# The early TensorE order written out by hand, first values by a one-hot matmul, and w_in loaded by columns

## The chip, the cores and the metric

The kernel runs on one core of a Trainium2 chip. The metric is the device time of one execution in microseconds (us); smaller is better. The four runs of the kernel before took 231.32, 231.59, 231.93 and 228.98 us, with a median of 231.45 us.

## What is computed

Attention over a sliding window with a few sink tokens, followed by a feed-forward layer. Four sequences (batches) of 768 tokens, eight heads of 64 columns. Each query sees the 128 keys up to its own position and the first four keys of its sequence. The result, 3072 tokens by 512 columns, goes through a gated layer with 2048 hidden columns. Cut to what matters:

```
scores = (q @ k.T) / sqrt(64)
keep   = (key < 4) | ((0 <= query - key) & (query - key < 128))
a      = softmax(where(keep, scores, -1e9))
x      = concat_heads(a @ v)                  # 3072 x 512
h      = x @ w_in                             # 3072 x 2048
g      = h * sigmoid(beta * h)
out    = g @ w_out                            # 3072 x 512
```

All inputs and the output are float32 in HBM; the kernel casts to bfloat16 for its matmuls.

## The kernel before

**Units.** The work is cut into eight half batches of 384 tokens (`hb`), and each into four head pairs. A pair of one half batch is a unit `u`, 32 of them, `u = 4 * hb + pair`. For a unit the kernel does these steps, each a group of instructions on TensorE with its followers on other engines:

- `T(u)` (L594): six transposes of q and k, 128 by 128, into one PSUM bank, and one copy of 768 columns to `qkT`, by ScalarE (ACT) or VectorE (DVE).
- `SC(n)` (L657): a burst of score matmuls. Each tile covers two PSUM banks; an exponential of 1024 columns on ACT writes `E`, and masks zero what may not be seen: for blocks with sink columns a product with `maskS` on DVE or GpSimd (POOL), for diagonal and previous blocks an `affine_select` of 512 columns on POOL (L703). One burst of each half batch also holds the scores of the sink keys for all four units (`SS`, L710), with an exponential into `ES`.
- `AV(u)` (L736): probabilities times values, 65 columns a matmul (64 values and a one that gives the denominator). Queries that lie beyond the first blocks take the sinks by one matmul of `ES` with `vS` (L746). A reciprocal and a product on DVE normalise (L761, L763).
- `OT(u)` (L769): three transposes of the result and a copy to `xT`.
- `HQ(T_, m)` (L793): for one token half `T_` and one of 16 chunks of 128 hidden columns, four matmuls of 384 columns, a tanh on ACT (L806) and a gate product on DVE (L808). Below, H0, H1 and so on are these in order.
- `OQ(T_, t, j)` (L815): four matmuls of 512 columns, a quarter of one output tile; after the fourth quarter a copy and a store. Below, O.

In the rest of the text T4, S5, A4, R4 are `T(4)`, `SC(5)`, `AV(4)` and `OT(4)`.

**First values.** `vS` holds the values of the four sink tokens, placed so that each head only meets its own rows. `load_first` (L552) fetches them from HBM in four loads of 8 KB for all batches, into a buffer zeroed by POOL (L468); `first_values` (L557) multiplies by the 0/1 array `own` on DVE, once for each batch.

**Loads.** All come from the SyncE (SP) queue, in program order. q and k of half batch 0 come in four loads of two heads each, those of half batches 1 and 2 in one load each of 768 KB; v in three loads of 256 KB with rows of 256 bytes. Weights come in 16 loads of 512 KB: `load_w(j)` (L512) for j < 8 takes half the depth of w_in and 512 of its columns (rows of 2 KB), for j >= 8 two row blocks of w_out. `cast_w(j)` casts on ACT, DVE or POOL, whichever the planner finds free first. An H therefore waits for two loads. The list is in L844: half batch 0, half batch 1, all weights, then the rest. The sink values' loads are put in after half batch 0.

**Order.** The program adds its operations to a graph; half batch 0 in an order written out (L979 to L1002), the rest by a loop (L1009 on) that picks the next group by expected readiness. `Graph.arrange` (L124) then plans every engine's queue from written-in durations: TensorE's next group is the earliest ready of the first `SKIP` = 3 in the list. While half batch 0 waits, filler matmuls of `ones` (L1003) go in. PSUM has eight banks; `take` gives the run of banks that is free first. The queues are fixed when the kernel is built, and TensorE works strictly in its order.

## Time and profile before

| | us |
|---|---|
| median of four runs | 231.45 |
| the profiled execution | 231.32 |
| its span, first to last instruction | 229.4 |
| TensorE (PE) busy | 215.4 (94%) |
| ACT busy | 142.8 (62%) |
| DVE busy | 139.2 (61%) |
| POOL busy | 65.3 (28%) |
| SP queue's transfers, share of the 16 DMA engines' span | 73.2% |
| H matmuls, 512 of 384 columns, busy | 95.1 |
| O matmuls, 360 records of 512 columns, busy | 90.3 |
| fillers, 54, busy (1.1 to 19 us) | 9.8 |

Times in the profile are counted from the start of the span. Matmuls overlap in their pipeline, so the mean duration of one (326 ns for H's) is longer than the distance from one start to the next. The chain that ended last lies on TensorE for 83% of the span, on transfers of k for 6%, on ACT for 4%. A line of a timeline gives the start, the length, the engine, the code line, the operation, the output and input with shapes, the count, and in brackets how long the engine sat idle before it and who ended that. The slices are fortieths of the span, 5.7 us each; a digit is a busy share in tenths.

### The profile page before, as it was taken

What the parts mean: (1) busy time and instruction counts of PE and PEld (TensorE: products, weight loads), DVE (VectorE), ACT (ScalarE), POOL (GpSimd) and SP (SyncE); (2) the same over time, 40 slices, a digit from 0 to 9 for tenths busy, and PEclk for the clock granted to TensorE, in tenths of its full rate; (3) what the DMA queues carried; (4) which work ended last, traced back from release to release, by engine and by line L of the source; (5) the groups of instructions that cost most, each with busy time, mean ns of one, the idle gap of its engine ahead of it and who ended that gap; (6) DMA issues with size and microseconds to landing.
All of it is one profiled execution on the core that took longest, in us unless ns stands there. A gap on an engine that the chain in (4) does not pass through costs nothing.

```text
span 229.4 us, 4562 instructions
## 1 busy us (share of the span) xinstructions
PE 215.4 (94%) x1771; PEld 125.3 (55%) x1795; DVE 139.2 (61%) x293; ACT 142.8 (62%) x226; POOL 65.3 (28%) x118
## 2 busy tenths in 40 slices
PE   7974989999899999999999999999999999999993
PEld 5662666554546456555655555656555565555541
DVE  2794559997686356567966563776765554533310
ACT  2844897775881487827667479672767864744421
POOL 5463493003262044407200046360120750000000
PEclk9997699999999999999999999999999999999999
DMA  6969699999985996987746995999669523011112
GB/s 168 244 197 334 175 357 367 334 300 236 197 199 113 246 237 96 201 197 148 153 87 160 223 212 96 225 189 163 135 117 209 182 80 83 0 46 49 47 48 90
DMA packets 95158, 39.79 MB, mean 174 GB/s; under 512 B 81809, under 2 KB 87969, under 8 KB 95137
## 3 DMA queue, kind: packets, MB, share of 16 engines
q1 hardware_dynamic: 95136, 39.51, 73.2%
q8 instruction: 14, 0.23, 0.4%
q14 instruction: 8, 0.06, 0.1%
HBM read 27.30 MB, written 6.29 MB: 146 GB/s over the span
## 4 chain that ended last, share of the span: by engine, by line
PE 83%; DMA 6%; ACT 4%; DVE 2%; issue 1%; SPq 1%; POOL 1%
PE P L801 36%; PE P L821 35%; DMA k_stage<-in_k_dram 6%; PE P L757 4%; PE P L678 4%; ACT E L690 2%; PE P L602 2%; PE P L746 1%; ACT qkT L444 1%; SPq L554 1%; DVE w_in L449 1%; POOL E L703 1%; DVE g L808 1%; PE P L783 1%; DVE k L449 1%
## 5 line engine op out<-in xcount | busy, mean ns | idle before, releaser
L806 ACT ACTIVATE t<-P,hbeta 128x384 f32<-128x384 f32 x128 | 72.9, 585 | 39.3 <-PE P L801 31.2
L808 DVE SCALAR_TENSOR_TENSOR g<-t,P 128x384 bf16<-128x384 f32 x128 | 68.7, 549 | 46.5 <-ACT t L806 43.4
L801 PE MATMUL P<-xT,w_in 128*128 128x384 bf16 x512 | 95.1, 326 | 0.7 <-ACT E L690 0.5
L821 PE MATMUL P<-w_out,g 128*128 128x512 bf16 x360 | 90.3, 379 | 1.7 <-issue 0.6
L703 POOL TENSOR_SCALAR_AFFINE_SELECT E<-E 128x512 bf16<-128x512 bf16 x72 | 48.8, 705 | 78.5 <-ACT E L690 78.4
L801 PEld LDWEIGHTS P<-xT,w_in 128*128 128x128 bf16 x512 | 48.2, 98 | 37.4 <-DVE w_in L449 0.9
L821 PEld LDWEIGHTS P<-w_out,g 128*128 128x128 bf16 x384 | 36.5, 98 | 36.4 <-DVE w_out L449 0.3
L690 ACT ACTIVATE E<-P 128x1024 bf16<-128x1024 f32 x44 | 43.0, 1031 | 10.2 <-PE P L678 9.9
L444 ACT ACTIVATE osb<-P 128x512 f32<-128x512 f32 x19 | 11.4, 599 | 20.1 <-PE P L821 19.6
L763 DVE TENSOR_TENSOR onorm<-P,rden 128x384 bf16<-128x384 f32 x32 | 17.8, 556 | 1.0
L757 PE MATMUL P<-vaug,E 128*128 128x65 bf16 x352 | 17.1, 193 | 0.2 <-POOL E L703 0.2
L757 PEld LDWEIGHTS P<-vaug,E 128*128 128x128 bf16 x352 | 15.6, 97 | 2.4 <-POOL E L703 0.3
L678 PE MATMUL P<-qkT 64*128 64x128 bf16 (+1 forms) x288 | 14.9, 237 | 0.6 <-ACT E L690 0.3
L678 PEld LDWEIGHTS P<-qkT 64*128 64x128 bf16 x288 | 9.8, 97 | 8.3 <-issue 2.6
L746 PE MATMUL P<-vS,ES 128*128 128x130 bf16 x64 | 12.8, 220 | 1.5 <-DVE vS L560 1.1
L449 DVE CAST k<-k_stage 128x512 bf16<-128x512 f32 (+1 forms) x19 | 9.6, 511 | 6.7 <-DMA k_stage<-in_k_dram 6.7
L761 DVE RECIPROCAL rden<-P 128x6 f32<-128x6 f32 x32 | 6.0, 188 | 10.9 <-PE P L757 10.8
L446 POOL TENSOR_SCALAR_AFFINE_SELECT q<-q_stage 128x512 bf16<-128x512 f32 x6 | 4.8, 814 | 26.1 <-DMA q_stage<-in_q_dram 26.1
L449 DVE CAST vaug<-v_stage 128x512 bf16<-128x512 f32 x21 | 9.9, 474 | 3.2 <-DMA v_stage<-in_v_dram 3.2
L1003 PE MATMUL P<-ones 128*128 128x256 bf16 x54 | 9.8, 331 | 1.1 <-POOL ones L455 1.1
L444 ACT ACTIVATE qkT<-P 128x768 bf16<-128x768 bf16 x9 | 7.0, 811 | 6.1 <-PE P L602 6.1
L698 DVE TENSOR_TENSOR E<-E,maskS 128x512 bf16<-128x512 bf16 x16 | 9.1, 580 | 2.3 <-ACT E L690 2.1
(50 smaller groups left out, 93.3 us busy)
## 6 DMA issues: line engine op xcount, KB each, us to landing
v_stage<-in_v_dram SPq DMA_DIRECT2D x24, 256.0 KB, 4.4
out_dram<-osb SPq DMA_DIRECT2D x24, 256.0 KB, 2.4
q_stage<-in_q_dram SPq DMA_DIRECT2D x15, 256.0 KB, 4.9
k_stage<-in_k_dram SPq DMA_DIRECT2D x15, 256.0 KB, 4.9
wst<-in_moe_w_in_dram SPq DMA_DIRECT2D x5, 512.0 KB, 9.3
wst<-in_moe_w_out_dram SPq DMA_DIRECT2D x4, 512.0 KB, 4.5
g<-in_moe_w_out_dram SPq DMA_DIRECT2D x4, 512.0 KB, 5.2
q_stage<-in_q_dram SPq DMA_DIRECT2D x2, 768.0 KB, 6.6
```

What stands on the lines that cost most here:

```text
L444: return lambda e: e.activation(dst, src, AF.Copy, bias=0.0, scale=scale)
L449: return lambda e: e.tensor_copy(dst, src)
L678: add("pe", lambda e, dst=dst, kt=kt, kc=kc, rows=rows, q0=q0, nq=nq, u=u: e.matmul(dst, kt[rows, kc:kc + 128], qkT[rows, u % NT, 0, q0:q0 ...
L690: add("act", lambda e, src=src, dst_=dst_: e.activation(dst_, src, AF.Exp, bias=0.0, scale=SCALE), act_ns(1024), w=[("E", z)] + [("m", z, ...
L703: add("gp", lambda e, dd=dd, sg=sg: e.affine_select(dd, dd, [[0, 4], [sg, 128]], ALU.is_ge, 0.0, base=min(sg, 0), channel_multiplier=-sg), ...
L746: add("pe", lambda e, m=m, c0=c0: e.matmul(A[:, c0:c0 + 2 * (D + 1)], ES[u // 4 % 2][:, m * 128:(m + 1) * 128], vS[b % 2][:, 2 * hp:2 * hp ...
L757: e.matmul(A[:, c0:c0 + D + 1], E[t_ % NE][:, i, hh, :], vaug[vz][:, kb % NK, 2 * hp + hh, :], start=a, stop=o, skip_group_check=True), 31,
L763: add("dve", lambda e: e.tensor_tensor(onorm[on][:, :, :, :].rearrange("p m h d -> p (m h) d"), av[:, :, 0:D], rden[on][:, :].unsqueeze(2) ...
L801: add("pe", lambda e, c=c: e.matmul(hp, w_in16[:, c, m * 128:(m + 1) * 128], xT[:, c, t0:t0 + HALF], start=(c == 0), stop=(c == 3)), mm_ns ...
L806: add("act", lambda e: e.activation(tt[ti][:, :], hp, AF.Tanh, bias=0.0, scale=hbeta[:, m:m + 1]), act_ns(HALF) + 93, r=["hbeta"], w=[("t" ...
L808: add("dve", lambda e: e.scalar_tensor_tensor(gt[T_ % NG][:, m, :], tt[ti][:, :], 1.0, hp, ALU.add, ALU.mult), dve_ns(HALF), r=[("t", ti)] ...
L821: add("pe", lambda e, m=m: e.matmul(P[:, bk, :], gt[T_ % NG][:, m, t * 128:(t + 1) * 128], w_out16[:, m, :], start=(m == 0), stop=(m == NM ...
```

## The change

Six things change.

1. **The early order.** For half batch 0 the list is T0 T1 S0 T2 S1 T3 S4 S2, the first values, S3, then A0 A1 R0 A2 R1 A3 R2 R3. After it stands a new written list of H, T and S for the next stage. For the first 60 us of the plan `arrange` may choose among ten groups, not three. In the resulting TensorE order H0 to H7 directly follow R3, then T4 to T7, then H8, S5, H9, and so on; the last part of the order, from the last attention unit on, is as before. PSUM banks of this stage are dealt out from written lists (`ring`, `two`).
2. **First values of batch 0** by one matmul with the 0/1 matrix `sel` from the values that are already in the vaug buffer; the product with `own` then reads PSUM. For batches 1 to 3 one load of 32 KB each, later in the queue.
3. **w_in loads** take the full depth and 256 columns (rows of 1 KB), so that an H waits for one load. w0, w1, w2 go ahead of half batch 1's q, w3 between its q and k, w4 and w5 between k and v; the `chain` argument keeps the order. beta's load moves behind w1. The first three casts have a fixed engine.
4. **T for the first two half batches** uses two banks and two copies of 384 columns.
5. **Diagonal and previous masks** of units 0 to 7 may also run on DVE, as a product with `maskT`.
6. **Output tiles of token half 0** go quarter by quarter over three tiles, and q and k heads 4 to 7 of half batch 0 come in one load each.

The diff, cut to its core:

```
     SKIP = 3
+    WIDE, EARLY = 10, 60000
...
-            for i, grp in enumerate(todo_pe[:self.SKIP]):
+            for i, grp in enumerate(todo_pe[:self.SKIP if self.free["pe"] > self.EARLY else self.WIDE]):
...
+        add("gp", lambda e: e.memset(sel[:, :], 0.0), 80, w=["sel0"])
+        add("gp", lambda e: e.tensor_copy(
+            sel[:, :].rearrange("p (h w) -> p h w", w=16)[:, :, 0:NSINK],
+            ident[:, 0:NSINK].unsqueeze(1).to_broadcast([128, H, NSINK])), 150, r=["sel0", "ident"], w=["sel"])
...
-            src = w_in_src[:, 2 * h:2 * h + 2, m * 512:(m + 1) * 512]
+            src = w_in_src[:, :, j * 256:(j + 1) * 256]
...
-        any_of(copies(dst, src_, {"act": 947, "dve": 602, "gp": 1060}), r=[("wst", j % NWS)], w=[("w16", m, h)])
+        src_ = wst[j % NWS].rearrange("p c f -> p (c f)").rearrange("p (c f) -> p c f", c=4 if m < 4 else 2)
+        any_of(copies(dst, src_, {"act": 947} if j == 0 else {"gp": 1060} if j < 3 else {"act": 947, "dve": 602, "gp": 1060}), r=[("wst", j % NWS)], w=[("w16", m, h)])
...
-    def load_first(s_):
-
-        add("sp", lambda e: e.dma_start(vS32[s_:128:16, :, :], v[:, :, s_, :].rearrange("b h d -> h b d")), 60,
-            r=["vS32z"], w=[("vS32", s_)], dma=f"ds{s_}")
+    def load_first(b):
+
+        add("sp", lambda e: e.dma_start(vS32[:, 0, :], v[b, :, 0:16, :]), 100,
+            w=["vS32"], dma="ds")
...
+    def first_values_pe():
+
+        G.begin()
+        bk = take(1)
+        add("pe", lambda e: e.matmul(P[:, bk[0], :], sel[:, :], vaug[0][:, 0, :, 0:D], start=True, stop=True), mm_ns(512),
+            r=["sel", ("v", 0, 0)], x=[("B", bk[0])])
+        add("dve", lambda e: e.tensor_tensor(
+            vS[0][:, :, 0:D], P[:, bk[0], :].rearrange("p (h d) -> p h d", d=D),
+            own[:, :].unsqueeze(2).to_broadcast([128, H, D]), ALU.mult), dve_ns(H * D),
+            r=["own", ("vSo", 0)], w=[("vS", 0)], x=[("B", bk[0])])
+        give(bk)
...
-        bs = take(1)
-        mp = P[:, bs[0], :].bitcast(BF16)
+        bs = take(1) + (take(1) if hb < 2 else [])
...
+                    tri = maskT[:, (1 - sg) // 2:(3 - sg) // 2, :].to_broadcast([128, 4, 128])
...
+                    if TILES[t_][0][1] < 8:
+                        alts["dve"] = (lambda e, dd=dd, tri=tri: e.tensor_tensor(dd, dd, tri, ALU.mult), 335)
...
-                r=[("w16", m // 4, c // 2), ("xT", c, T_ % NXT)], x=[("B", bs[0])])
+                r=[("w16", m // 4, m // 2 % 2), ("xT", c, T_ % NXT)], x=[("B", bs[0])])
...
-    LOADS = xl(0) + xl(1) + list(range(16)) + [x for hb in range(2, NSB) for x in xl(hb)]
+    x1 = xl(1)
+    LOADS = xl(0) + [0, 1, 2] + x1[:1] + [3] + x1[1:2] + [4, 5] + x1[2:] + list(range(6, 16))
+    LOADS += [("f", 1)] + [x for hb in range(2, NSB) for x in xl(hb) + ([("f", hb // 2 + 1)] if hb in (3, 5) else [])]
...
-    OS = [(T_, t, j) for T_ in range(NSB) for t in range(3) for j in range(4)]
+    OS = [(0, t, j) for j in range(4) for t in range(3)]
+    OS += [(T_, t, j) for T_ in range(1, NSB) for t in range(3) for j in range(4)]
...
+    for x in "T0 T1 S0 T2 S1 T3 S4 S2 V S3".split():
+        if x == "V":
+            cast(0, "v", 0)
+            first_values_pe()
+        else:
+            {"T": T, "S": SC}[x[0]](int(x[1:]))
...
+    for name, i in [("A", 0), ("A", 1), ("R", 0), ("A", 2), ("R", 1), ("A", 3), ("R", 2), ("R", 3)]:
+        step(name, i)
...
+    ring[0] = [7, 6, 5, 4]
+    early = "H0 H1 H2 H3 H4 T4 T5 T6 T7 H5 S5 H6 H7 S6 H8 S7 H9".split()
+    for x in early:
+        if x == "H0":
+            beta_in()
```

## The prediction

> **What bounds the kernel now.** I read first the forty slices of the span, then the order in time of TensorE, of SyncE's queue and of ScalarE over the first 60 us, then windows of 2 us, then the chain of waits.
>
> ```profile
> PE   7974989999899999999999999999999999999993
> ...
> PEclk9997699999999999999999999999999999999999
> ...
> GB/s 168 244 197 334 175 357 367 334 300 236 197 199 113 246 237 96 201 197 148 153 87 160 223 212 96 225 189 163 135 117 209 182 80 83 0 46 49 47 48 90
> ```
>
> TensorE is full from the seventh slice (about 34 us) to the last but one. Nothing that shortens another engine's work there can matter much. The weak part is the head, slices 3 to 6, with the clock down in 4 and 5. The order of TensorE in time there:
>
> ```profile
> 13.87 0.34 PE L757 MATMUL P<-vaug,E 128*128 128x65 bf16 x6
> 15.36 0.22 PE L746 MATMUL P<-vS,ES 128*128 128x130 bf16 x1 [1.14 <-DVE vS L560]
> ...
> 19.26 0.33 PE L602 MATMUL P<-ident,q 128*128 128x128 bf16 x3
> 22.39 0.80 PE L602 MATMUL P<-ident,k 128*128 128x128 bf16 x3 [2.80 <-DVE k L449]
> ...
> 29.21 1.47 PE L801 MATMUL P<-xT,w_in 128*128 128x384 bf16 x8 [0.52 <-ACT E L690]
> ```
>
> The first half batch is attended by 19.2. TensorE then wants the second half batch's keys, waits 2.80 us, runs transposes and scores slowly, and starts the first feed-forward matmul (H0) only at 29.21. Why the keys are late, from SyncE's queue and the windows (fourth to last columns: clock, DMA share, GB/s):
>
> ```profile
> 8.92 3.00 SPq L554 DMA_DIRECT2D vS<-in_v_dram  x4
> 11.96 0.45 SPq L510 DMA_DIRECT2D q_stage<-in_q_dram  x1
> 12.46 1.36 SPq L510 DMA_DIRECT2D k_stage<-in_k_dram  x1
> ...
> 15.29 9.05 SPq L510 DMA_DIRECT2D v_stage<-in_v_dram  x3
> ```
>
> ```profile
> 12.00:14.00 2.00, 2.00 (x31) 1.68 (x31) 2.00 (x4) 1.95 (x3) 1.55 (x3) 1.00 0.33 51
> ...
> 20.00:22.00 2.00, 0.00 (x0) 0.00 (x0) 0.09 (x1) 0.09 (x1) 0.06 (x1) 0.64 1.10 359
> 22.00:24.00 2.00, 1.58 (x13) 1.31 (x14) 0.46 (x2) 1.30 (x2) 1.64 (x2) 0.50 0.84 183
> 24.00:26.00 2.00, 2.00 (x25) 1.56 (x22) 1.77 (x3) 1.53 (x4) 0.26 (x1) 0.50 0.49 112
> ...
> 36.00:38.00 2.00, 2.00 (x28) 1.48 (x25) 1.93 (x7) 1.65 (x4) 0.19 (x1) 1.00 1.00 377
> ```
>
> Four loads of 8 KB hold SyncE for 3.0 us, and the transfers have run dry by 12 to 14 (51 GB/s). A second hole (22 to 26) lies behind the v loads, whose issue took 9.05 us. Otherwise the transfers are as full as TensorE: 28 to 46 averages 352 GB/s. So the first 58 us have two limits, TensorE's order and bytes.
>
> **What the Trainium skill says.** "TensorE: Matmul & The Clock Gate", Part 1: an idle array falls to half clock and comes back after some 3.4 us of work. The trace agrees in kind: 0.50 from 21 to 27, though TensorE worked again from 22.4, so some 5 us. The same page, "Back-to-back issue gap", gives N/2.4 + 2.5 ns: 162 ns for 384 columns, 216 for 512. The chain has eight of the first in 1.30 us and four of the second in 0.86: agreed. "DMA: Bandwidth & Descriptors", Specifications: rows of 512 B and more go at line rate. The v loads (256 B rows) ran at 205 to 229 GB/s between 25 and 28, the 2 KB weight rows at 352; 1 KB rows don't occur here.
>
> **The change, part by part.**
>
> *Warm prices on TensorE* from the chain: H (four matmuls of 384) 0.65, a quarter of an output tile (O) 0.86, three transposes 0.17, one unit of attention-times-values (A) 0.54. T4-T7 are 8 x 0.17 = 1.4; the scores S5-S8 are 40 matmuls at 0.55/12 each, and 0.17 for the sinks: 2.0. Together 3.4 us, for which 19.26 to 29.21 took 9.95. So 6.5 us are lost, 3.9 to waits (2.80, 0.26, 0.30, 0.52, rounded) and the rest to the half clock.
>
> *The written order* puts H0-H7 (8 x 0.65 = 5.2 us) in that gap; they need 1024 of w_in's columns, which are four loads of 256 columns. In the old split two half-depth loads had to land for 512 columns. TensorE's order after the change is H0-H7, T4-T7, then H8, H9, H10 among S5-S8 and A4.
>
> *The head.* The tiny loads go from SyncE (3.0 us), one zeroing from GpSimd (0.30, hidden: GpSimd is idle from 4.2 to 6.6), and both early vS products from VectorE (2.15). Added: two GpSimd constants (0.2 to 0.3 each, same idle stretch), one 512-column matmul (0.22) and one vS product from PSUM (0.7, the row's faster value). This removes the 1.14 wait. ScalarE then binds: five exponentials at 0.93, ES 0.28, five split copies at 0.45 and two casts at 0.5 are 8.2 us from about 5.0, with a wait for heads 4 to 7 (landed about 9). The last exponential ends near 14.2 against 13.77; its mask on VectorE takes 0.5 where GpSimd needed until 15.7. Four normalisations at 0.69, as now, and one mask between them: the last ends near 17.8, transpose and copy 0.7, so **H0 at about 18.7**. Bounds 17.5 (no wait) and 20.0 (as now: 19.09 + 0.2 + 0.5).
>
> *ScalarE afterwards.* Up to the copies of R4 (the transpose of unit 4) its order holds 13 tanh at 0.51, 6 exponentials at 0.93, ES 0.4, 2 casts at 0.53, 5 split copies at 0.45: 15.9 us from about 19.5 (H0's end), the last exponential three tanh before the end, at 33.9. A7 and R4 follow at 35.2. TensorE's own work up to there is 13 x 0.65 + 3.4 + 4 x 0.54 + 0.17 = 14.2, that is 32.9. So a new loss of 2.2 us. Late there: A6 and A7, waiting for exponentials. Moving masks from GpSimd to VectorE removes what ended this stage before (GpSimd solid from 27.0 to 35.2).
>
> *Output tiles of the first token half* are walked by quarter of w_out, so three PSUM banks stay held and five are left. One H holds a bank for about 0.65 + 0.58 (tanh) + 0.55 (gate) us, under three banks at a time; I price this at nothing, and if a bank is late, H waits where O matmuls stood. Two-bank transposes with split copies add 8 ACT or VectorE instructions, counted above.
>
> *The transfers.* x of the first half batch (2.36 MB) is in by about 11.3, as now. Then in the new order: w0-w2 1.57 MB at 340 (a choice between the v rows' 215 and 352, close to the upper end), 15.9; q1 0.79 MB at 330 (14 to 20 now), 18.3; w3, 19.9; **k1, 22.3** (now 21.9, and TensorE is ready at 18.7 + 5.2 = 23.9: free); w4, w5, 25.4; v1 at 215, 29.0, or 30 with half of a hole like that of 22 to 26; then w6-w15 5.24 MB at 350, 45.0; q2 and k2, 49.8. Now k2 lands at 55.8, so about 6 us earlier: the holes of 2.7 and 2.0 us (missing bytes at 300 GB/s) and better filling. Small beta and later vS loads (one of 32 KB each in place of the four) are nothing beside this.
>
> *Where it ends.* The next place where TensorE must wait for bytes is T8 (now its keys' transpose is at 58.22). Ahead of it, after H0, stand 19 H, 11 O, 3.4, A4-A7 2.2, R4-R7 0.7: 28.1 us. 18.7 + 28.1 + 2.2 = 49.0, while k2 and its cast give 50.4. So bytes decide: **T8 at 50.4**. Now 28 H and 7 O stand ahead of T8, 24.2 us against 21.8, so 2.4 us of work move behind. Behind T8 remain 229.4 - 58.2 = 171.2. Sum: 50.4 + 171.2 + 2.4 = 224.0; 0.4 for small new waits of a changed order (none to 2 possible, each sign); 224.4. Outside the span lie 231.32 - 229.4 = 1.9: 226.3, and the profiled run stands 0.13 under the median: **226.4 us**. The tail is the same order (two H, 36 matmuls of O).
>
> **Rivals.** *More than that* (0.18): TensorE, not bytes, decides at T8, and the head or ScalarE is better than worked out: T8 near 47, so 222.5 to 223. For it: H0 could be 17.5. Against: 14.7 MB up to k2. *Bytes later* (0.20): holes like those now seen open again behind v1, with SyncE blocked as in its 9.05 us: k2 at 53 to 54, T8 at 54, 229.5 to 230. *Slower* (0.07): rows of 1 KB move like 256 B ones. w_in's 4.19 MB at 215 take 19.5 us, not 12.3: k1 comes at 26, TensorE cools again, and T8 is at 57.6, which gives 233.6. It decides from about 250 GB/s downwards with one further hole: T8 beyond 55.8 eats the whole gain. *The one-hot matmul brings nothing* because values land no sooner: H0 at 19.7, still before bytes decide; the forecast stays.
>
> **How the numbers follow.** Forecast 0.55, its own range 224 to 228.5. One per cent (2.3 us) is about what can be told from no change. Faster by more: all of the first rival, nearly all of the forecast, a third of the second: 0.77; within 0.15; slower 0.08. The range runs from the first rival's end to the second's: 222.4 to 230.2.
>
> **What would show it.** H0 near 18.7 directly after the first half batch's last transposes; clock 1.00 through 20 to 28; no window under 100 GB/s between 12 and 26; exponentials, not GpSimd, ending A6's and A7's waits; T8 waiting for k near 50. Wrong if TensorE idles over 2 us before T4 (k1 behind w_in), if the clock falls there, or if k2 lands past 54.

## The result, and the profile after

The changed kernel takes 231.9 us (median of 43 runs, 229.5 to 234.6), the kernel before in the same sessions 229.8 (64 runs, 227.9 to 233.5). The ratio is 1.0089, with a 95% interval of 1.0069 to 1.0108: some 2 us slower, where 5 us less was forecast. The 231.45 us of the first four runs stood 1.6 us over the kernel's usual time, because its executions differ in the clock that TensorE was granted. Of some 250 that came with the experiments, 79 had a mean clock of 0.995 or more and a median of 228.3 us, 104 about 0.99 and 230.15, and 67 less and 231.2. The profiled one (0.984) was of the last kind. Of 44 runs of the changed kernel 31 had 0.995 or more (231.5 us), and none less than 0.99.

So at a full clock the change costs 3.2 us (231.5 against 228.3), more than the medians say; it holds the full clock in 70% of its executions, the kernel before in 32%. And an execution of the kernel before at full clock is some 2.9 us ahead of the profiled one (231.2 - 228.3, an estimate), without any change. Every lead below is over the profiled one and has to be read with that in mind.

The profiled execution of the changed kernel took 231.86 us, with a span of 230.1. Its slices (fortieths of the span, busy share in tenths):

```profile
PE   8798787999999999999999999889999999999993
...
PEclk9999999999999999999999999999999999999998
...
GB/s 160 253 329 364 244 283 391 388 247 227 166 119 229 242 99 101 219 205 193 87 131 255 220 112 120 153 225 175 131 116 257 80 80 48 0 46 46 50 46 91
```

The dip of the clock in slices 4 and 5 is gone, and so are the small transfer rates of slices 3 and 5. TensorE is softer now in slices 5 to 7, and there is a new soft place in slices 26 and 27, 144 to 155 us. The head, in TensorE's order of time:

```profile
18.00 0.34 PE L842 MATMUL P<-ident,onorm 128*128 128x128 bf16 x3 [0.35 <-DVE onorm L822]
18.18 3.68 PE L860 MATMUL P<-xT,w_in 128*128 128x384 bf16 x20
22.13 0.82 PE L860 MATMUL P<-xT,w_in 128*128 128x384 bf16 x4 [0.27 <-DVE g L867]
24.17 1.47 PE L860 MATMUL P<-xT,w_in 128*128 128x384 bf16 x8 [1.21 <-DVE g L867]
25.48 0.33 PE L649 MATMUL P<-ident,q 128*128 128x128 bf16 x3
```

H0 starts at 18.18, directly behind the last transposes. The 1.21 us ahead of H6 (24.17) is put down to a gate product, and one did end at 24.11. But the gates were late because VectorE had casts of late loads ahead of them: it waited 0.72 us for q of half batch 1 (landed at 21.16) and then for the fourth load of w_in, w3, issued at 12.46 and landed only at 22.47.

```profile
22.49 0.69 DVE L476 CAST w_in<-g 128x1024 bf16<-128x1024 f32 x1 [0.42 <-DMA g<-in_moe_w_in_dram]
23.10 1.94 DVE L867 SCALAR_TENSOR_TENSOR g<-t,P 128x384 bf16<-128x384 f32 x4
```

The rows of 1 KB are not the reason: the windows of 2 us (last columns: clock, DMA share, GB/s) show them at 355 to 377 GB/s.

```profile
18.00:20.00 2.00, 1.91 (x13) 1.07 (x14) 0.11 (x2) 1.30 (x4) 1.06 (x1) 1.00 1.09 377
20.00:22.00 2.00, 1.86 (x12) 0.89 (x10) 1.28 (x3) 1.34 (x3) 0.78 (x1) 1.00 1.10 355
22.00:24.00 2.00, 0.82 (x4) 0.31 (x4) 1.58 (x4) 1.55 (x4) 0.13 (x1) 1.00 1.09 375
```

At T8 no transfer is waited for:

```profile
52.84 0.33 PE L649 MATMUL P<-ident,q 128*128 128x128 bf16 x3
53.01 0.33 PE L649 MATMUL P<-ident,k 128*128 128x128 bf16 x3
```

The kernel before did wait there for its keys:

```profile
58.22 0.34 PE L602 MATMUL P<-ident,k 128*128 128x128 bf16 x3 [0.57 <-DVE k L449]
```

**Where the lead went.** To compare kernels whose groups stand in another order, I count TensorE's own work: each matmul by its warm price (0.16 us for one of H, 0.215 for one of O, 0.05 for a score, and so on, 200.7 us in all), and note when each trace has begun as much. The lead is the time by which a kernel is ahead of the first profile of before at equal work. For the changed kernel it is 5.0 us at 12 us of work (27.6 us of time), 2.1 at 24 (43.5), 2.9 at 36, just past T8 in both, 1.9 at 60 and still 1.9 at 120 (141.9); then 0.85 at 126, -0.2 at 132, -0.5 at 150, -1.1 at 156, and -1.0 at the end. (Where H and O stand in another order, slightly other prices move a lead: the one at 36 us of work lies between 2 and 2.9. Those at 120 and at the end hold to 0.3.) The whole gain of the head is lost, in two places: half of it up to 44 us, and 2.9 us between 142 and 181, where the code is the same as before. TensorE there:

```profile
143.24 1.47 PE L860 MATMUL P<-xT,w_in 128*128 128x384 bf16 x8 [0.44 <-ACT E L745]
...
147.90 0.39 PE L880 MATMUL P<-w_out,g 128*128 128x512 bf16 x1 [0.63 <-DVE g L867]
...
149.43 0.34 PE L816 MATMUL P<-vaug,E 128*128 128x65 bf16 x6
150.73 0.23 PE L805 MATMUL P<-vS,ES 128*128 128x130 bf16 x1 [0.96 <-DVE vS L594]
```

The attention A24 (first unit of half batch 6) waits for `vS`. VectorE, in the same window, waits for the values to land and has everything else behind that wait, the gate products too:

```profile
146.95 0.43 DVE L476 CAST vaug<-v_stage 128x512 bf16<-128x512 f32 x1 [0.91 <-DMA v_stage<-in_v_dram]
147.30 1.01 DVE L867 SCALAR_TENSOR_TENSOR g<-t,P 128x384 bf16<-128x384 f32 x2
149.64 0.43 DVE L476 CAST vaug<-v_stage 128x512 bf16<-128x512 f32 x1 [1.33 <-DMA v_stage<-in_v_dram]
149.98 0.69 DVE L594 TENSOR_TENSOR vS<-vS,own 128x512 bf16<-128x512 f32 x1
```

And why they land so late is in SyncE's queue, where the three loads stand one by one between transposes of the output:

```profile
138.75 1.27 SPq L836 DMA_TRANSPOSE xT<-onorm  x1
140.06 0.58 SPq L541 DMA_DIRECT2D v_stage<-in_v_dram  x1
140.69 2.56 SPq L836 DMA_TRANSPOSE xT<-onorm  x2
143.29 0.58 SPq L541 DMA_DIRECT2D v_stage<-in_v_dram  x1
143.92 2.35 SPq L836 DMA_TRANSPOSE xT<-onorm  x1
146.31 0.57 SPq L541 DMA_DIRECT2D v_stage<-in_v_dram  x1
146.93 0.67 SPq L588 DMA_DIRECT2D vS<-in_v_dram  x1
```

Before, the same loads stood together, and a little later in time:

```profile
143.98 2.19 SPq L510 DMA_DIRECT2D v_stage<-in_v_dram  x3
...
147.19 2.51 SPq L777 DMA_TRANSPOSE xT<-onorm  x2
```

They landed there by 149.6, exactly as in the changed kernel. But A24 came at 155.6 there, and comes at 149.4 here. Before:

```profile
155.58 0.34 PE L757 MATMUL P<-vaug,E 128*128 128x65 bf16 x6
155.76 0.22 PE L746 MATMUL P<-vS,ES 128*128 128x130 bf16 x1
```

### The profile page after: what moved, and what is told of

It is laid out like the page before. It is cut to its first block, busy times and chain, and to the rows that moved or that the text cites. A ratio compares the mean times of both kernels' runs of the same rounds, so it can differ in the third digit from the quotient of the medians.

```text
span 230.1 us, 4524 instructions
## 1 busy us (share of the span) xinstructions
PE 214.9 (93%) x1762; PEld 122.7 (53%) x1787; DVE 137.9 (60%) x289; ACT 150.3 (65%) x246; POOL 62.6 (27%) x111
## 4 chain that ended last, share of the span: by engine, by line
PE 64%; DVE 9%; DMA 9%; SPq 8%; ACT 6%; issue 1%
PE P L880 31%; PE P L860 26%; DMA v_stage<-in_v_dram 4%; DMA g<-in_moe_w_in_dram 4%; SPq L541 4%; DVE g L867 3%; PE P L733 3%; PE P L816 3%; ACT E L745 3%; SPq L836 3%; DVE onorm L822 2%; ACT qkT L471 2%; ACT t L865 1%; DVE E L763 1%; PE P L805 1%
## 5 line engine op out<-in xcount | busy, mean ns | idle before, releaser
L860 PE MATMUL P<-xT,w_in 128*128 128x384 bf16 x512 | 98.6, 326 | 3.8 <-DVE g L867 3.1
L880 PE MATMUL P<-w_out,g 128*128 128x512 bf16 x359 | 92.2, 379 | 2.3 <-issue 0.6
L759 POOL TENSOR_SCALAR_AFFINE_SELECT E<-E 128x512 bf16<-128x512 bf16 x63 | 43.4, 710 | 89.2 <-ACT E L745 88.8
L745 ACT ACTIVATE E<-P 128x1024 bf16<-128x1024 f32 x44 | 43.5, 1036 | 4.4 <-PE P L733 4.4
L471 ACT ACTIVATE osb<-P 128x512 f32<-128x512 f32 x23 | 13.7, 597 | 13.5 <-PE P L880 13.3
L816 PE MATMUL P<-vaug,E 128*128 128x65 bf16 x352 | 17.6, 193 | 0.9 <-DVE vaug L476 0.4
L476 DVE CAST q<-q_stage 128x512 bf16<-128x512 f32 (+1 forms) x16 | 7.6, 476 | 6.6 <-DMA q_stage<-in_q_dram 6.3
L1071 PE MATMUL P<-ones 128*128 128x256 bf16 x45 | 8.7, 342 | 1.1 <-POOL ones L482 1.1
L471 ACT ACTIVATE qkT<-P 128x384 bf16<-128x384 bf16 (+1 forms) x12 | 6.0, 543 | 3.8 <-PE P L649 3.8
L471 ACT ACTIVATE k<-k_stage 128x512 bf16<-128x512 f32 (+1 forms) x10 | 6.3, 625 | 3.3 <-DMA k_stage<-in_k_dram 3.1
```

The lines of the kernel that those rows point to most:

```text
L471: return lambda e: e.activation(dst, src, AF.Copy, bias=0.0, scale=scale)
L476: return lambda e: e.tensor_copy(dst, src)
L745: add("act", lambda e, src=src, dst_=dst_: e.activation(dst_, src, AF.Exp, bias=0.0, scale=SCALE), act_ns(1024), w=[("E", z)] + [("m", z, ...
L759: alts = {"gp": (lambda e, dd=dd, sg=sg: e.affine_select(dd, dd, [[0, 4], [sg, 128]], ALU.is_ge, 0.0, base=min(sg, 0), channel_multiplier= ...
L816: e.matmul(A[:, c0:c0 + D + 1], E[t_ % NE][:, i, hh, :], vaug[vz][:, kb % NK, 2 * hp + hh, :], start=a, stop=o, skip_group_check=True), 31,
L860: add("pe", lambda e, c=c: e.matmul(hp, w_in16[:, c, m * 128:(m + 1) * 128], xT[:, c, t0:t0 + HALF], start=(c == 0), stop=(c == 3)), mm_ns ...
```

## The experiments

All of them edit one of the two kernels; most by a pass over the finished plan that moves single operations to another place or engine (`dv0`, `dv1` are the loads of values of even and odd half batches, of which the fourth belong to half batches 6 and 7; `ds` the sink values; `do` the stores). Ratios are to the kernel before, with 95% intervals. Leads are those of one trace each; kernels that are alike up to there differ by up to 1.6 us in the head from trace to trace (4.4 to 6.0 at 12 us of work), so the loss from 120 us of work to the end tells more than the lead itself.

| run | median us (runs) | ratio | lead at 12 / 24 / 120 / end |
|---|---|---|---|
| the changed kernel | 231.9 (43) | 1.0089 [1.0069, 1.0108] | 5.0 / 2.1 / 1.9 / -1.0 |
| p1_v_first | 233.3 (6) | 1.0171 [1.0105, 1.0238] | 4.4 / 1.9 / 1.7 / -3.7 |
| p3_v6_first | 231.0 (22) | 1.0067 [1.0036, 1.0099] | 4.4 / 1.2 / 1.0 / -1.0 |
| p4_v_act | 232.0 (6) | 1.0109 [1.0057, 1.0162] | 5.3 / 2.0 / 1.8 / -1.2 |
| p5_v6_sp_v7_act | 232.2 (6) | 1.0109 [1.0059, 1.0158] | 5.9 / 3.5 / 3.3 / 0.6 |
| p2_masks_pool | 232.15 (6) | 1.0118 [1.0056, 1.0181] | 3.9 / 0.3 / 0.1 / -1.3 |
| p6_no_masks | 230.3 (12) | 1.0033 [1.0001, 1.0065] | 6.6 / 4.7 / 3.2 / 0.4 |
| q1_av_late | 230.0 (22) | 1.0026 [0.9998, 1.0053] | 5.3 / 2.9 / 2.6 / 1.4 |
| q2_stores_pool | 230.15 (22) | 1.0031 [1.0004, 1.0058] | 6.0 / 3.6 / 3.0 / 2.3 |
| q7_av_late_stores_pool | 229.55 (22) | 0.9995 [0.9966, 1.0023] | 4.6 / 2.0 / 1.4 / 1.0 |
| c1_before | 230.7 (18) | 1.0021 [0.9987, 1.0055] | 0.6 / 0.1 / 0.1 / 0.1 |
| b1_warm | 229.8 (22) | 1.0046 [1.0016, 1.0076] | 1.7 / 1.7 / 1.7 / 1.7 |
| b2_onehot | 229.1 (22) | 0.9987 [0.9959, 1.0015] | 3.8 / 3.4 / 3.5 / 2.0 |
| b5_columns | 230.9 (13) | 1.0044 [1.0021, 1.0068] | 4.8 / 2.4 / 0.1 / 0.1 |
| b3_onehot_v_act | 228.4 (22) | 0.9943 [0.9919, 0.9967] | 3.1 / 2.7 / 2.8 / 2.1 |
| b4_v_act_early | 232.9 (18) | 1.0107 [1.0075, 1.0139] | 4.2 / 2.7 / 2.8 / -2.0 |
| q3_onehot_stores_pool | 228.15 (22) | 0.9949 [0.9921, 0.9977] | 3.8 / 2.2 / 1.9 / 1.8 |
| q4_onehot_v7_pool | 228.4 (22) | 0.9970 [0.9942, 0.9997] | 3.8 / 3.4 / 3.5 / 3.4 |
| q6_onehot_v7_fill | 228.2 (22) | 0.9938 [0.9913, 0.9964] | 4.3 / 3.9 / 4.0 / 3.9 |

### The late loss: moving the value loads

First SyncE's queue alone: the value loads of half batches 6 and 7 ahead of the transposes (p1), then only those of half batch 6 (p3).

```diff
+        for o in [o for o in new if o.dma and (o.dma[:2] == "dv" or o.dma == "ds")]:
+            seen[o.dma] = seen.get(o.dma, 0) + 1
+            if seen[o.dma] < (3 if o.dma == "ds" else 4):
+                continue
...
+            for i in reversed(sp):
+                if new[i].dma[:2] not in ("xo", "do"):
+                    break
+                to = i
+            new.insert(to, new.pop(at))
```

> The changed kernel, but on SyncE's queue alone the value loads of half batches 6 and 7 stand ahead of the output transposes (four DMA transposes of 1.27 us issue each) that they were mixed with; nothing else moves. Theory A (the late loss is this mixture): the waits at 143, 148, 151 us and at 176 us go, TensorE keeps the lead of about 1.9 us over the kernel before that it has at 142 us, so 2.5 to 3.5 us less than the changed kernel, ratio 0.985 to 0.990 to it, about 0.993 to the kernel before. Theory B (the late loss lies with VectorE or with banks, whatever the order of the loads): within 0.5 us of the changed kernel, ratio to before about 1.007.

> The changed kernel; on SyncE's queue only the value loads of half batch 6 (and the sink values that follow them) stand ahead of the output transposes they were mixed with; half batch 7 stays as in the changed kernel. Theory A (the mixture of half batch 6 costs 2.5 us at 143 to 151 us; what went wrong in the run with both moved was half batch 7's, which made the last transposes late): those waits go, the wait of 0.45 us at 176 stays, 2 to 2.5 us less than the changed kernel, ratio to before 0.998 to 1.003. Theory B (the output transposes are then late here as well): a new wait of H for xT, total as in the changed kernel or longer.

With p1 the waits at 143 to 151 shrank to one of 0.44 us, and the lead went from 1.7 at 120 us of work to 1.35 at 144. But then, on TensorE:

```profile
166.91 0.35 PE L793 MATMUL P<-qkT,kS 128*32 128x384 bf16 x4
170.19 0.82 PE L878 MATMUL P<-xT,w_in 128*128 128x384 bf16 x4 [2.94 <-ACT osb L489]
```

```profile
169.54 0.60 ACT L489 ACTIVATE osb<-P 128x512 f32<-128x512 f32 x1 [4.87 <-DMA out_dram<-osb]
```

Half batch 7's loads had gone ahead of a store too: it was issued at 165.31 and landed at 169.52 (163.75 and 166.22 in the changed kernel). ScalarE's copy into its buffer waited for it, TensorE waited for the bank that this copy frees, and the clock fell (slice 30 of that run shows 0.7). The two lost 5.2 us. (The output transposes were later as well, the first at 169.8 in place of 166.7, but this H does not read them: its four matmuls follow one another while the last of them lands at 172.5.) With p3 the first part of the gain is there again (1.0 at 120, 0.5 at 150) without that, but the waits for half batch 7's values at 175 to 176 grew from 0.45 to 1.27 us, and the lead ended where the changed kernel's does. Theory A was right for the first place and wrong for the total: these values land at 173 to 175.2 in either run, and a TensorE that comes earlier only waits longer.

Then the same loads on ScalarE's queue: both half batches (p4), or half batch 6 as in p3 and half batch 7 on ScalarE, issued 27 us earlier than in the changed kernel (p5: 142.8 to 143.9, in place of 169.5 to 170.8).

```diff
+                if seen[o.dma] >= (3 if o.dma == "ds" else 4):
+                    o.eng = "act"
```

> The changed kernel; the seven loads of values and sink values of half batches 6 and 7 are issued from ScalarE's queue, at their place in the plan, instead of SyncE's; nothing else moves. SyncE is issuing without a pause from 124 to 173 us, and a transpose holds it for 1.27 us. Theory A (SyncE's queue is what gives the lead back): no wait for values after 140 us, SyncE done about 4 us earlier with the transposes of half batch 7, the lead of 1.9 us stays to the end, 2.5 to 3.5 us less than the changed kernel, ratio to before 0.993 to 0.998. Theory B (bytes, since the queue's work is all transfer; or ScalarE, which pays 0.6 us for each issue, becomes late with tanh): less than 1 us gained.

> The changed kernel; half batch 6's values stand ahead of the output transposes on SyncE as in p3_v6_first, and half batch 7's three value loads are issued from ScalarE's queue beside SyncE's loads of that half batch's q and k, some 17 us earlier than before; their staging buffer has long been free. Theory A (the loss after 140 us is the late landing of values, at 143 to 151 and again at 174 to 176 us): no wait for values after 140 us, no loss of lead from 120 to 186 us of work but 0.5, so 1.3 us less than p3_v6_first, median 229.5 to 230.2, ratio to before 0.998 to 1.002. Theory B (without these waits others of the same size come up, since ScalarE, VectorE or the transposes of the output are as late): within 0.5 us of p3_v6_first.

Neither gained (the trace of p5, at 230.2 us, is of the fastest of its six runs; their median is 232.2). In p4 SyncE was indeed through with its transposes 2.3 us earlier, but the loads on ScalarE landed at 141.3, 146.2 and 148.0 for half batch 6, and at 171.2 to 175.3 for half batch 7: they stand behind exponentials and tanh there, took up to 2.2 us to issue, and moved at the same time as four stores. In p5 no wait for values is left at all, and the loss came back in one piece elsewhere:

```profile
149.38 0.34 PE L889 MATMUL P<-xT,w_in 128*128 128x384 bf16 x1 [2.10 <-DMA xT<-onorm]
```

The early loads (issued at 142.8 to 143.9) ran together with the transposes of the output, which then landed 4.0 to 5.6 us after their issue. The last two of the four took 4.7 and 5.6 us; in p3, which is the same but for these loads, 3.3 and 2.4. The DMA engines were fuller too: their share in windows of 2 us from 144 to 150 us is 1.2 to 1.3 in p5 and 0.3 to 0.65 in p3. So a load taken out of SyncE's way can still be in the way of the next transfer.

### The late loss: the order and the queue

What differs from before is the order: on the same scale of work A24 stands at 123.1 us in the changed kernel, at 128.5 before and at 131.5 with the one-hot alone; A28, the first unit of half batch 7, at 147.2 against 154.6 and 154.6. The planner has put the same attention 5.4 and 7.4 us of work earlier than before, while SyncE, whose queue is occupied for 96% of the time from 57 to 173 us (before: 92%), is hardly earlier. q1 moves only the attention, by one line of the planner; q2 only relieves SyncE; q7 does both.

```diff
             t, tb = G.at(av_keys(i)), banks_at(1)
+            if t is not None and i in (24, 28):
+                t += 3000
```

```diff
+        stores = [o for o in new if o.dma and o.dma[:2] == "do"]
+        for o in stores[:15]:
+            o.eng, o.dma = "gp", o.dma + "g"
```

> The changed kernel with one line more in the planner: the first attention units of half batches 6 and 7 (A24, A28) count as ready 3 us later than they are, and the plan is made anew. A24 then stands at 126.8 us of TensorE's work (123.1 in the changed kernel, 128.5 before), A28 at 155.9 (147.2 and 154.6). Theory A (attention stands too early in the order for its values, which come at a time that SyncE's queue sets): no wait over 0.5 us between 140 and 180 us, the lead at 120 us of work is kept to within 0.7 us, total 2 to 3 us less than the changed kernel, ratio to before 0.995 to 1.000. Theory B (SyncE's or VectorE's work, whatever the order): lead lost as before, within 0.7 us of the changed kernel.

> The changed kernel; the first fifteen stores of the output are issued by GpSimd in place of SyncE, every order left as it is. They hold SyncE for about 1 us each, some 8 to 10 us of its queue up to 165 us. Theory A (SyncE's full queue gives the time at which values and transposes are in): the value loads of half batch 6 land 2 us or more earlier, the waits at 143 to 151 us shrink below 1 us in sum, total 1.5 to 2.5 us less than the changed kernel. Theory B (SyncE waits for the data of its transposes, not for its turn; or GpSimd's masks come late behind its own stores): loads no earlier, total within 0.7 us or longer.

> The changed kernel with both edits of q1_av_late and q2_stores_pool. Theory A (the two together are the late loss): less than 0.5 us of lead lost from 120 us of work to the end (2.9 in the changed kernel, 1.3 and 0.7 with one), no wait over 0.5 us after 140 us, median 229 to 229.6, ratio to before 0.996 to 0.999. Theory B (one cause, and each edit finds the same gain): as q1 and q2, ratio 1.002 to 1.003.

All three took away most of the late loss. Behind 120 us of work it is 2.9 us in the changed kernel, 1.3 in q1, 0.7 in q2 and 0.4 in q7, and no wait of TensorE after 140 us is longer than 0.44 us in any of them. In q2 the values of half batch 6 landed at 139.0 to 145.4, in the changed kernel at 143.3 to 149.6. Theory A of q1 had said more, a loss of 0.7 us at most and a ratio of 1.000 or less. In q7 SyncE and TensorE, in order of time, read so:

```profile
136.81 5.15 SPq L843 DMA_TRANSPOSE xT<-onorm  x4
142.01 2.04 SPq L548 DMA_DIRECT2D v_stage<-in_v_dram  x3
144.09 0.96 SPq L595 DMA_DIRECT2D vS<-in_v_dram  x1
```

```profile
151.97 1.03 PE L887 MATMUL P<-w_out,g 128*128 128x512 bf16 x4
152.83 0.34 PE L823 MATMUL P<-vaug,E 128*128 128x65 bf16 x6
153.01 0.22 PE L812 MATMUL P<-vS,ES 128*128 128x130 bf16 x1
```

A24 stands 3.4 us later than in the changed kernel, ordinary O and H matmuls fill the time, and A24 waits for nothing. The medians follow: 231.9, then 230.0 and 230.15, then 229.55, a ratio of 0.9995 [0.9966, 1.0023]. So the cause of the late loss is shown: attention that comes early meets a queue that delivers late, and it is enough to mend either side. That both edits together do more than one is not shown: the intervals of the three ratios overlap, and at a full clock the medians are 229.5 (q1), 229.9 (q2) and 229.4 us (q7). What is left of the change then equals the kernel before by the medians; at a full clock it is still about 1 us slower (229.4 against 228.3).

### The head: clock, one-hot, columns, masks

> The kernel before, unchanged, for a second trace. Theory A (its 43 runs shown so far fall into groups by granted clock, with a median of 228.1 us at 0.995 and over and of 231.05 us under 0.990, so the first profile caught a rare one): clock 0.99 or more, no window at half clock between 20 and 28 us, keys of half batch 1 in earlier than 21.9 us or the gap before them too short for the clock to fall, H0 near 26, T8 near 55, span 226 to 228. Theory B: half clock from 20 to 27 us again and a span near 229.4.

The kernel before once more, unchanged. Theory A fell. The keys of half batch 1 landed 1.2 us earlier (20.65 against 21.88), the gap before them was 2.00 us at a full clock, and the clock fell all the same, only later:

```profile
26.00:28.00 2.00, 1.27 (x15) 0.54 (x10) 0.71 (x2) 2.00 (x3) 2.00 (x4) 0.65 0.91 279
28.00:30.00 2.00, 2.00 (x9) 0.99 (x8) 0.00 (x0) 2.00 (x4) 2.00 (x4) 0.50 1.03 366
```

So the half clock is no accident but the commoner case (171 of 250 executions have less than 0.995). The Trainium skill, "TensorE: Matmul & The Clock Gate", Part 1, says that the window in which activity is watched runs freely, and that the number of slow matmuls at the start of one and the same kernel differs from run to run. For a fall inside the kernel these traces agree in kind: b2 and q3 (below) have the same order up to 30 us and the same two waits, of 0.8 us each, at 28.5 and 30.0; q3 has half clock from 30.1 on, b2 a full clock. No trace of the kernel before with a full clock was had.

b1 puts 24 fillers of 256 columns into the gap of 2.80 us.

```diff
+        for n in range(24):
+            o = Op()
+            o.eng, o.dma, o.ns, o.x, o.preds = "pe", None, 110, [bank], []
+            o.fn = self.warm(bank[1])
...
+            new.insert(at, o)
```

> The kernel before with 24 filler matmuls of 256 columns (into an idle bank) in the gap of 2.80 us between the query and the key transposes of unit 4, so that TensorE does not fall idle there; the order of all else is the same. Theory A (the half clock from 20 to 27 us is an accident of some executions, and costs those 2 to 3 us): clock 1.00 in every run, times without the upper group at 231.5 us, the median about 228 us, 0.990 to 0.995 of before. Theory B (the half clock is in all runs of before, or costs nothing since the wait for the bytes of T8 swallows it): the ratio to before is 0.985 or lower in the first case, 1.00 in the second.

Slower than before by 0.5%. In its trace the keys had landed at 19.13, but the fillers ended at 21.74. The same load landed at 21.88, 20.65 and 19.13 in three traces of this order, so a gap of one trace is no constant. The fillers did keep the clock full more often (16 of 22 runs), but at a full clock b1 takes 229.7 us, where the kernel before takes 228.1 in its session: in executions that would not have lost the clock, work of fixed length in the gap only costs.

b2 is the one-hot matmul alone, in the kernel before: its diff is the two parts `load_first` and `first_values_pe` shown with the change, with `sel`. b5 adds the column loads and the mixed list of loads (the diff is against b2).

```diff
-    LOADS = xl(0) + xl(1) + list(range(16)) + [("f", 1)]
+    x1 = xl(1)
+    LOADS = xl(0) + [0, 1, 2] + x1[:1] + [3] + x1[1:2] + [4, 5] + x1[2:] + list(range(6, 16)) + [("f", 1)]
```

> The kernel before with the one-hot matmul alone: the four loads of 8 KB are gone from the head and their 3.0 us of SyncE with them, the sink values of batches 1 to 3 come by one load each later; the list of loads, the written order and the masks stay, the planner orders the rest. Theory A (the tiny loads cost because SyncE issues nothing else meanwhile): the keys of half batch 1 land 2 to 3 us earlier, the gap of 2.80 us shrinks to under 0.5, H0 starts near 26; of this at most 1 us is left at T8 and at the end, 228 to 230 us. Theory B (the transfers are bound by bytes, not by issue): the keys land within 1 us of 21.9, H0 stays near 29, the total within 0.5 us of before.

> The kernel before with the one-hot matmul, and with w_in loaded by columns in the changed kernel's list (three weight loads ahead of q of half batch 1, one between q and k, two between k and v); no written order, no masks on VectorE, T as before; the planner orders the rest. Theory A (the mixed list alone makes the early feed-forward possible, and k1 comes later for it): H0 near 19 as in the changed kernel, keys of half batch 1 in at 23 to 25 us; lead at 24 us of work 2 to 3 us, less than the one-hot alone (3.4). Theory B (columns help): lead at 24 and 36 us of work over 3.7 us.

The one-hot alone brings the keys in at 18.65, H0 to 23.15 and a lead of 3.4 us at 24 us of work, more than the whole change has there (2.1), and 19 of its 22 runs have a clock of 0.995 or more. At a full clock, though, it takes 228.8 us, no less than the kernel before (228.1 in its session): what it has is a full clock in more of the executions. It loses 1.4 us of it late, at 178 to 182, again to values of half batch 7. b5 has H0 at 18.97 and T4's keys at 26.36 behind a wait of 1.59 us: a lead of 4.8 at 12 and 2.4 at 24 us of work, much like the changed kernel's. So the mixed list gives the early H and takes it back by 43 us; the written order adds nothing that these traces show. (b5 then lost 1.7 us at 95 to 101 us to score banks and gate products, an order of its own.)

p2 moves the eight masks of units 4 to 7 from VectorE to GpSimd; p6 leaves them out, all but one column of each, so that its output is no longer the layer's.

```diff
+            if o.tri and o.eng == "dve":
+                o.eng = "gp"
+                o.fn, o.ns = o.alts["gp"]
```

> The changed kernel, but the eight diagonal and previous masks of units 4 to 7 that the plan put on VectorE are done by GpSimd, at the same place in the order. Theory A (VectorE, 1.9 to 2.0 us busy in every 2 us from 30 to 42 us, is what slows this stretch): the lead at 24 us of TensorE work grows from 2.1 to 3 or 4 us, the total falls by 0.5 to 2 us. Theory B (ScalarE's exponentials, or bytes, set the pace): the lead at that place stays at 2.1 us or shrinks, the total stays within 0.5 us of the changed kernel or is up to 2 us longer, GpSimd being slower at a mask.

> The changed kernel, with the eight diagonal and previous masks of units 4 to 7 on VectorE cut to one column (the other columns are left unmasked), so that some 4.5 us of VectorE's work between 29 and 38 us are gone. Theory A (VectorE bounds that stretch): the four waits for g and E there (2.0 us) go, the lead at 24 us of work grows from 2.1 to 3.5 us or more, and as much is left at 48. Theory B (ScalarE, full from 26 to 36 us, or bytes): the waits take other names and the lead at 24 to 36 us of work stays within 0.5 us.

On GpSimd they cost: A6 and A7 waited 2.3 us for masks between 35 and 41 us, and 3.6 us of lead were lost from 12 to 24 us of work. Left out, the loss from 12 to 24 us of work is 1.95 us, where the eight traces with the changed kernel's order there lose 2.4 to 3.3. So VectorE's masks are 0.5 to 1.3 us of it (an estimate, p6 being one trace). The rest was not taken apart: in the changed kernel ScalarE too is busy for 2.00 of every 2 us from 26 to 36 us, and bounds by ScalarE and by VectorE are not told apart here.

### A version that beats both

b3 and b4 put value loads of the one-hot version on ScalarE's queue, as p4 and p5 do for the changed kernel; q3 moves its stores to GpSimd, q4 half batch 7's values alone (`o.eng, o.dma = "gp", o.dma + "g"` for the fourth `dv1`); q6 is q4 with six of b1's fillers.

> The kernel before with the one-hot matmul alone, and the value loads of half batches 6 and 7 issued from ScalarE's queue. With the one-hot alone the lead over the profiled run of before was 3.4 to 3.7 us up to 178 us, then 1.8 us of it went, with values of half batch 7 landing late (waits of 0.99 and 0.45 us). Theory A (SyncE's queue): that 1.8 us stays, median 227 to 227.6 us, ratio to before 0.990 to 0.994. Theory B (bytes, or ScalarE): within 0.5 us of the one-hot alone, ratio 0.998.

> As b3_onehot_v_act, with the three value loads of half batch 7 issued from ScalarE some 17 us earlier, beside the loads of that half batch's q and k. Theory A (late values are what is left of the loss): no wait for values at 178 to 182 us, lead over the profiled run of before 2.7 to 3.5 us at the end in place of 2.1, median 227.5 to 228, ratio to before 0.988 to 0.992. Theory B: the wait of 0.49 us for a score bank and one of 0.4 for g stay and take it, ratio 0.993 to 0.996.

> The kernel before with the one-hot matmul alone; the first fifteen stores of the output are issued by GpSimd. Theory A (SyncE's queue): values of half batch 7 land 1 us or more earlier, the waits of 0.99 and 0.45 us at 178 to 182 us go, ratio to before 0.990 to 0.994. Theory B: GpSimd late with masks, ratio 0.998 or more.

> The kernel before with the one-hot matmul alone; only the three value loads of half batch 7 are issued by GpSimd, at their place in the plan. Theory A (they are late because they stand behind six transposes on SyncE): they land 2 us or more earlier than 175.6 to 179.2, the waits for them go and no wait for a score bank takes their place (GpSimd does no copies there), 1 to 1.8 us less than the one-hot alone, ratio to before 0.990 to 0.994. Theory B (bytes, or GpSimd's slower issue): land no earlier, ratio 0.998.

> The version q4_onehot_v7_pool (one-hot alone, values of half batch 7 issued by GpSimd) with six filler matmuls of 256 columns ahead of the first key transposes of half batch 1, 0.65 us, about the wait there. Theory A (the idle 0.7 us tips TensorE into half clock in half of the executions, at 0.7 us each): fewer runs at a clock of 0.99, median 227.7 to 228.2, ratio to before 0.991 to 0.995. Theory B (the half clock starts elsewhere, in the first 12 us; the fillers only delay the keys): clocks as before, median 228.4 to 228.9.

b4 was a clear miss. Half batch 7's three early loads held ScalarE for 3.8 us, its exponentials came late, and VectorE, which waited for them, had half batch 6's value casts and the `vS` product behind that wait:

```profile
150.01 3.78 ACTq L532 DMA_DIRECT2D v_stage<-in_v_dram  x3
153.84 2.85 ACT L724 ACTIVATE E<-P 128x1024 bf16<-128x1024 f32 x3 [3.24 <-issue]
154.89 0.43 DVE L732 TENSOR_TENSOR E<-E,maskS 128x512 bf16<-128x512 bf16 x1 [4.62 <-ACT E L724]
```

A24 then waited 2.19 us for `vS`, and 4.8 us were lost. q3 and q4 lost 0.1 us late in place of 1.4. In q4 the values landed at 163.3 to 167.8, 11 to 12 us earlier than with the one-hot alone. In q3 they landed at 176.2 to 178.4, hardly earlier than there (175.6 to 179.2); its TensorE came to A28 1.5 us later, so its trace does not show that the stores were the cause. b3 lost 0.7: with the value loads beside it a store landed late, the copy that takes its buffer waited 1.28 us, and TensorE 0.49 us for the bank. q6 has a ratio of 0.9938 [0.9913, 0.9964], 228.2 us against 230.3 in its session; 15 of its 22 runs had a full clock, 12 of q4's, which is too few to call the fillers' part shown. At a full clock q3 takes 227.3 us (kernel before in its session: 228.2), q6 227.8 (228.6), b3 228.1 (228.25) and q4 228.15 (228.2). So q3 and q6 are faster in themselves by some 0.5 to 1 us; the rest of what the medians show is a full clock in more of the executions. Whether an emptier SyncE queue helps the kernel before without the one-hot was not tried. The slices of q6:

```profile
PE   8988889998999999999999999999999999999993
...
PEclk9999999999999999999999999999999999999999
```

## Why the prediction was wrong

The sum was 50.4 us up to T8, 174.0 behind it (171.2 + 2.4 + 0.4) and 2.0 outside the span. Measured were 52.8, 177.3 and 1.8. So 2.4 us were lost up to T8 and 3.3 behind it.

- **The head** was right: H0 at 18.18 (forecast 18.7; 17.7 to 20.2 over the variants), directly behind the transposes, clock full through 20 to 28, no window under 100 GB/s between 12 and 26.
- **The transfers** came 2.4 us late at k1 (24.70 for 22.3) and 2.6 at w3 (22.47 for 19.9), at the full rate foreseen. The values of half batch 0 were in at 12.56, not at "about 11.3, as now"; they landed at 12.35 before as well, so that was misread. And the step summed bytes in order of issue: up to k1 these are 3.67 MB, while the windows from 12.56 to 24.70 hold some 4.3 MB (an estimate from the rates of the 2 us windows), so loads behind k1 had a share before it was complete. They did not overtake it. The Trainium skill, "DMA: Bandwidth & Descriptors", Queues, rings and completion order, says that the DMAs of one issuing engine need not complete in the order of issue; here, from w0 to v1, all landed in that order. The price, by way of VectorE's casts, was 1.5 us of waits ahead of T4.
- **ScalarE's loss of 2.2 us** ahead of A6 and A7 has the right size, by luck: four waits between 29 and 39 us make 1.95, but three are put down to gate products and one to a mask, all on VectorE, not to exponentials. That the masks on VectorE would clear this stage was half right: on GpSimd they cost more (p2), but they are part of what fills VectorE (p6).
- **T8** was not decided by bytes: k2 had landed at 51.15 (49.8 forecast), and TensorE was busy up to T8. From H0 on it needed 34.7 us for 28.1 us of work, where 2.2 us of waits were allowed. Six waits make 3.4 us; the other 3 are in short ones and in matmuls that started late without an idle gap, and were not taken apart. The lead at T8 is 2.9 us; 58.2 - 50.4 - 2.4 made it 5.4.
- **The step that failed** most is the last one: "0.4 for small new waits of a changed order (none to 2 possible, each sign)", with 171.2 us behind T8 taken over from before. It measured 3.7 us (177.3 - 171.2 - 2.4), of which 2.9 lie behind 120 us of work; between T8 and there new waits of 0.5 us can be seen. The sum took it that what is planned behind T8 stays as it was. It doesn't: the plan moved A24 and A28 forward by 5.4 and 7.4 us of work, to where SyncE could not deliver. The profile of before had the warning: SyncE's queue, read only up to 60 us, is occupied for 92% of the time up to 173.
- **The base** was 1.6 us high, and the half clock was counted as a sure gain of 2.6; about a third of the executions don't have it. Against these a lead of 2 us up to 120 us of work is no gain at all, if the clock is all that differs: the changed kernel's 231.5 us at full clock less the late loss of 2.9 is 228.6, the kernel before 228.3.
- **Rivals**: none was the cause. The slower one (1 KB rows at 215 GB/s) is refuted by 355 to 377 GB/s, "bytes later" by k2's landing at 51.15 (53 to 54 foreseen), and the result is longer than the 229.5 to 230 that it gave.

## What to carry to other kernels

A lead won in the head of a planned kernel is worth only what the fullest in-order queue behind it can keep: read every queue, the DMA issuer's too, to the end of the span before a gain is carried to the end. Where a planner makes the order anew, compare the place of each consumer with the landing of its data far behind the change; moving two groups back by 3 us of plan and taking fifteen stores off SyncE won back 2.5 of 2.9 us, either alone 1.6 and 2.2. Try the smallest part of a change alone first: here the one-hot matmul had more lead at 24 us of work than the whole change, and with one queue relieved it was 0.3 to 0.6% faster than the kernel before. And where executions differ in the granted clock, compare those of one clock before a lead is called a gain: most of this head's lead was over a profile that had lost the clock.

## What the runs showed of the hardware

- A DMA transpose holds SyncE for 1.2 to 1.3 us and lands 2.3 to 2.5 us after its issue where little else moves (half batch 7 of the changed kernel); with loads of 256 KB beside it, 4.0 to 5.6 us (p5).
- A load of 256 KB issued by ScalarE among its other work took 0.4 to 2.2 us to issue and landed 3.1 to 6.8 us later (p4); three in a row took 3.8 us, and ScalarE stood still for 3.2 of them (b4). On GpSimd's queue a load took 0.9 to 1.1 us to issue and landed after 4.4 to 6.9 us, and TensorE waited for none of these values (q4).
- Half clock came in stretches of 3.4 us (c1, p2, q3) or 6.8 us (the profile of before, 20.6 to 27.4). In c1 it began 5.4 us after a wait of 2.0 us had ended, with three shorter waits (0.25 to 0.64 us) in between; in p2 0.6 us after one of 1.25 us; in q3 0.1 us after one of 0.83 us, which in b2 left the clock full. What decides was not tested.
